# Retention and wave-MLP kernel: some transposes as four 64 by 64 tiles, and the order from the ninth unit on

## The chip, the cores and the metric

The kernel runs on one core of one Trainium2 chip. The metric is the device time of one execution in microseconds (us). The core has a matrix engine (PE, with PEld for its weight loads), three engines for elementwise work (DVE, ACT, POOL) and SP, which here only issues DMAs. ACT and POOL issue DMAs too.

## The reference, cut to what matters

Inputs are q, k and v (4 batches, 8 heads, 768 positions, 64 per head) and four weights. The first part is a linear recurrence per head, the second a token and channel mixer on the result.

```
gamma = 1.0 - 2.0 ** (-5.0 - arange(8));  scale = 1/8
for t in range(768):                                   # per batch and head
    state = gamma * state + outer(k[t], v[t])
    y[t] = scale * (q[t] @ state)
x = y, laid out as (4, 768, 512)
theta = x @ w_theta
zr, zi = x * cos(theta), x * sin(theta)
u = x + w_tok_r @ zr + w_tok_i @ zi                    # over the 768 positions
out = u + max(u @ w_ch, 0)
```

## The kernel before, in words

The recurrence is computed in blocks of 256 positions. A **unit** n is one block of 4 heads of one batch; there are 24, two (the halves of the heads) for each block, three blocks for each batch. Each pair of units yields two **tiles** C of 128 positions by 512 channels, 24 in all, and the second part works on these. Matrix work is in bf16 with f32 sums in PSUM.

The whole program is a list written out by hand, ORDER (L22 to L85): each token names a function and its arguments, and a loop at the end (L616) calls them one after the other. The last letter of a token, where there is one, names the engine (p POOL, v DVE, a ACT) or the DMA queue (s SP, a ACT). The instructions of one engine run in the order of the list; a layer below puts in the waits between engines, for data and for buffers that are used again.

For a unit: Lk, Lq, Lv load its k, q, v; ck, cq (or cqs) and cv cast and scale them into kqb and vb. Tk and Tq transpose k and q on PE, four 128 by 128 transposes each, into one PSUM tile kq_ps, and E copies that to kqT in SBUF. In some units one DMA transpose, Dk, issued by SP, takes the place of Tk, Tq and E. A computes the scores from kqT, m masks them on DVE. ST computes the new state terms, S0 and S1 (DVE or ACT) add them up, SB copies the state to a block-diagonal tile. I and Y add the parts of the output in PSUM (r_ps, tags R0 and R1), and XA or XB copies it to xT, transposed.

For a tile: Tx and Ex (or the DMA transpose Dx) turn xT back into x; Hh multiplies by w_theta; CN (ACT) takes cosine and sine, z multiplies. M.t.s adds one of six terms of the token mix of tile t, two matmuls with 512 columns; u adds x. Tu and Eu (or the DMA transpose Du) transpose u to uT; O multiplies by w_ch; f applies the maximum and the sum; SO stores. Tw and Ew transpose one tile of 128 rows of w_tok_r or w_tok_i, six transposes and a copy. The last tile and tile 20 are handled in halves (Mh, uh, Tuh, Euh, Oh, fh, Oa, fa).

A, ST and Y work on 64 by 64 pieces: 16 matmuls each, with 64 rows and 64 stationary columns, and a stream of 128 columns (A, Y) or 64 (ST). All other PE work uses the full 128 by 128 array.

PSUM buffers: tag tr (two) for kq_ps, x_ps, u_ps, w_ps and a few o_ps; tag acc (two) for th_ps, y_ps, o_ps; R0, R1 and at one each. In SBUF kqT has four buffers, kqb and vb five, xT, u and ot four, uT three.

Names and lines that matter below: L316 kq_ps transposes, L346 A, L373 ST, L423 Y, L411 I, L455 x_ps, L491 w_ps, L521 u_ps, L469 Hh, L509 M, L536 O, L137 and L139 copies on ACT and on the other engines, L157 loads, L332 Dk, L462 Dx, L531 Du, L547 SO.

Of the kernel before, what the change touches and what calls it, by code (L numbers as in the profile page):

```python
# [16 lines left out]
BF = mybir.dt.bfloat16  # L17
# [54 lines left out]
cv.21.v u.14 A.21 ST.21 CN.19.0 CN.19.1 S0.21.v M.15.3 M.15.5 S1.21 m.21 XA.20.1 Hh.18 CN.18.1
CN.18.0 Dx.18 Dk.22 ck.23.a M.15.4 M.15.2 SB.21.0.p M.15.1 M.15.0 SB.21.1.v Lv.23.s Du.12 Dx.19
XA.20.0 O.9 f.9 I.21 Y.21 A.22 ST.22 M.16.1 cqs.23.p u.15 m.22 S0.22.v z.18.p z.19.p M.16.5
SB.22.0.p M.16.4 O.12 M.16.0 SO.8.a M.16.2 M.16.3 SB.22.1.p XB.21.0.a XB.21.1.a SO.11.s Du.14
cv.23.p Dk.23 f.12 Du.13 Dx.20 Dx.21 Hh.21 u.16 I.22 A.23 Y.22 ST.23 CN.21.0 CN.21.1 Hh.20 CN.20.1
S0.23.v XA.22.1 XA.22.0 SB.23.0.a M.17.1 M.17.3 CN.20.0 M.17.0 SB.23.1.p I.23 M.17.2 m.23 Y.23 O.13
M.17.4 z.21.v M.17.5 Mh.0.1 Mh.0.3 XB.23.1.v f.13 Hh.23 u.17 XB.23.0.a SO.13.a CN.23.1 Du.16 Hh.22
z.20.v CN.22.1 Mh.0.2 M.19.3 Dx.23 CN.23.0 Dx.22 Mh.0.0 M.21.1 M.19.1 z.23.p CN.22.0 SO.6.a Du.17
M.18.1 O.16 M.21.2 M.19.2 M.19.0 M.18.3 f.16 SO.9.a M.18.5 z.22.p M.18.2 O.17 M.19.4 M.18.0 Mh.0.4  # L80
M.18.4 f.17 u.18 Du.15 SO.12.s O.15 M.19.5 f.15 u.19 SO.16.s M.22.2 M.22.1 O.14 Mh.0.5 uh.0 f.14
M.22.0 M.21.5 M.22.3 M.22.5 Du.19 M.21.4 SO.17.s M.22.4 Du.18 O.19 M.21.0 M.21.3 M.20.2 Mh.1.2
Mh.1.0 Mh.1.4 u.22 O.18 Mh.1.3 SO.15.a f.19 M.20.0 M.20.1 Tuh.0 u.21 Du.22 Du.21 f.18 M.20.3 Euh.0
M.20.4 Mh.1.1 M.20.5 u.20 O.22 Mh.1.5 uh.1 f.22 Tu.20 SO.14.a SO.19.s Eu.20.a O.21 SO.18.a Tuh.1
Euh.1 f.21 Oa.0 Oa.1 fa.0 fa.1 Oh.0 Oh.1 SO.21.a SO.22.s SO.20.s fh.0 SOh.0 fh.1 SOh.1 Z.31  # L85
# [14 lines left out]
def kernel(  # L100
# [228 lines left out]

    def Dk(n):  # L330
        kqT = work.tile([P, 2, 2, 2, P], BF, name="kqT", bufs=4)
        nc.sync.dma_start_transpose(  # L332
            out=kqT.rearrange("p w a j t -> p (w a j) t"),
            in_=st["kqb", n].rearrange("p w d -> p (w d)"))
        st["kqT", n] = kqT

    def A(n):
        kqT = st["kqT", n]
        at_ps = psum.tile([P, 2, 2, 2, P], FT, name="at_ps", tag="at", bufs=1)
        for j in range(2):  # L340
            for a in range(2):
                for c in range(2):
                    cols = slice(c * D, (c + 1) * D)
                    for g in range(2):
                        rows = slice(g * D, (g + 1) * D)
                        nc.tensor.matmul(at_ps[cols, g, j, a, :],  # L346
                                         kqT[rows, 0, a, j, cols],
                                         kqT[rows, 1, :, j, cols],
                                         start=(j == 0 and a == 0),
                                         stop=(j == 1 and a == 1), skip_group_check=True)  # L350
# [55 lines left out]
    def I(n):  # L406
        _, i, h = unit(n)
        r = R_of(n + 1)
        for c in range(0 if i else 1, 2):
            for j in range(2):  # L410
                nc.tensor.matmul(r[c][:, j * P:(j + 1) * P], sbd_of(n)[:, c, j, :],  # L411
                                 st["kqT", n][:, 1, :, j, c * D:(c + 1) * D],
# [47 lines left out]

# [186 lines left out]
```

## Time and profile before

| | us |
|---|---|
| median of 3 runs | 165.23 |
| lowest, highest | 165.05, 165.78 |
| span of the profiled execution | 163.6 |

The span runs from the first to the last instruction of one profiled execution; the time of the runs holds what lies around it as well. The profile page gives busy time by engine, the same in 40 slices of the span, DMA queues, and the groups of instructions by line, with the number of them, the time of all, the mean of one in ns, and the idle time of the engine ahead of them with what ended it. Matmuls are pipelined: the busy time of one (0.38 us for 512 columns) is longer than the distance to the next (0.22 us). Lines starting with L give the line of the kernel, then engine, operation and tiles as out<-in; SPq is SP's queue of DMA issues, where a row's length is the time of the issue.

### The profile page before, as it was taken

To read this page: it belongs to the slowest core of one execution; us is meant where nothing else is said; L and a number is where in the kernel's file an instruction comes from. 1 tells how busy PE (TensorE), PEld (TensorE's weight loads), DVE (VectorE), ACT (ScalarE), POOL (GpSimd) and SP (SyncE) were. 2 spreads that over 40 slices of the span, in tenths; PEclk is the share of its full clock that TensorE was granted. 3 is DMA by queue.
4 is the path that set the end of the run, shared out by engine and by line. 5 is a ranking of instruction groups with operands and counts; after the bars stand their busy time and mean duration, and the time that the engine had idled before them with its cause. 6 is when DMAs were issued, how large, how long until landed. Compare 5 with 4: busy or idle time off the path is not lost.

```text
span 163.6 us, 4928 instructions
## 1 busy us (share of the span) xinstructions
PE 155.2 (95%) x2034; PEld 87.2 (53%) x2034; DVE 114.0 (70%) x215; ACT 78.9 (48%) x140; POOL 74.3 (45%) x107
## 2 busy tenths in 40 slices
PE   5996889999999999999999999999999999999992
PEld 1453655656666655654554565554545554444561
DVE  3388687887994895984879894887867760345372
ACT  4976697974658255773343726732341616000020
POOL 7557389075034552730227599950469204600000
PEclk9999999999999999999999999999999999999999
DMA  3999999999999999999999999999897548515546
GB/s 115 297 290 255 268 283 236 275 220 286 220 162 232 223 291 139 338 203 270 324 263 198 134 268 221 242 193 298 125 245 136 103 92 227 160 64 128 129 164 224
DMA packets 69062, 34.93 MB, mean 214 GB/s; under 512 B 26416, under 2 KB 66096, under 8 KB 69040
## 3 DMA queue, kind: packets, MB, share of 16 engines
q1 hardware_dynamic: 56032, 23.73, 69.4%
q10 hardware_dynamic: 10320, 7.47, 17.7%
q0 software_dynamic: 2688, 3.41, 12.1%
q8 instruction: 16, 0.26, 0.7%
q14 instruction: 6, 0.05, 0.1%
HBM read 25.69 MB, written 6.29 MB: 196 GB/s over the span
## 4 chain that ended last, share of the span: by engine, by line
PE 76%; DMA 8%; ACT 5%; POOL 3%; issue 2%; SPq 2%; DVE 1%; POOLq 0%; ACTq 0%
PE y_ps L509 36%; PE o_ps L536 11%; PE th_ps L469 10%; DMA kqf<-in_k_dram 8%; PE r_ps L423 3%; ACT qx L233 3%; PE w_ps L491 3%; PE at_ps L346 3%; PE r_ps L411 2%; PE kq_ps L316 2%; SPq L157 2%; PE y_ps L561 2%; ACT cs L476 1%; PE x_ps L455 1%; PE r_ps L373 1%
## 5 line engine op out<-in xcount | busy, mean ns | idle before, releaser
L509 PE MATMUL y_ps<-z,wtr 128*128 128x512 bf16 x138 | 52.4, 380 | 0.0
L509 PE MATMUL y_ps<-z,wti 128*128 128x512 bf16 x138 | 52.3, 379 | 0.0
L483 POOL TENSOR_TENSOR z<-cs,x_sb 128x1024 bf16<-128x1024 bf16 x12 | 25.5, 2136 | 17.9 <-ACT cs L476 10.0
L355 DVE TENSOR_TENSOR at<-at_ps,mask 128x1024 bf16<-128x1024 f32 x24 | 29.2, 1216 | 0.2
L469 PE MATMUL th_ps<-wth,xT 128*128 128x512 bf16 x96 | 24.5, 379 | 0.5 <-ACT cs L476 0.4
L516 DVE TENSOR_TENSOR u<-y_ps,x_sb 128x512 bf16<-128x512 f32 x23 | 15.8, 688 | 12.7 <-PE y_ps L509 12.6
L542 DVE SCALAR_TENSOR_TENSOR ot<-o_ps,u 128x512 f32<-128x512 f32 x22 | 15.1, 688 | 12.5 <-PE o_ps L536 12.4
L308 POOL TENSOR_TENSOR vb<-vf,vsc 128x512 bf16<-128x512 f32 x15 | 15.6, 1041 | 17.3 <-DMA vf<-in_v_dram 16.9
L476 ACT ACTIVATE cs<-th_ps,zerob 128x512 bf16<-128x512 f32 x24 | 16.4, 685 | 13.3 <-PE th_ps L469 8.8
L536 PE MATMUL o_ps<-wch,uT 128*128 128x512 bf16 x88 | 22.6, 379 | 0.0
L476 ACT ACTIVATE cs<-th_ps,halfpi 128x512 bf16<-128x512 f32 x24 | 16.3, 686 | 11.5 <-issue 5.4
L509 PEld LDWEIGHTS <-wtr 128*128 128x128 bf16 x138 | 13.5, 98 | 12.7
L509 PEld LDWEIGHTS <-wti 128*128 128x128 bf16 x138 | 13.5, 98 | 12.0 <-issue 0.2
L139 POOL CAST sbd<-s 64x256 bf16<-64x256 f32 (+1 forms) x21 | 10.1, 481 | 20.8 <-DVE s L391 17.7
L137 ACT COPY kqT<-kq_ps 128x1024 bf16<-128x1024 bf16 x12 | 12.1, 1012 | 11.9 <-PE kq_ps L316 11.9
L469 PEld LDWEIGHTS <-xT 128*128 128x128 bf16 x96 | 8.8, 98 | 8.7 <-issue 0.5
L137 ACT CAST kqb<-kqf 128x512 bf16<-128x512 f32 x16 | 9.6, 620 | 6.9 <-DMA kqf<-in_k_dram 6.3
L536 PEld LDWEIGHTS <-uT 128*128 128x128 bf16 x88 | 8.1, 98 | 8.3
L278 PE MATMUL zz<-zero 128*128 128x512 bf16 x30 | 10.3, 476 | 1.9 <-DVE zero L192 1.9
L423 PE MATMUL r_ps<-at,vb 64*64 64x128 bf16 x384 | 9.9, 221 | 1.6 <-DVE at L355 1.6
L316 PE MATMUL kq_ps<-ident,kqb 128*128 128x128 bf16 x120 | 11.2, 220 | 0.3 <-POOL kqb L302 0.3
L139 POOL CAST kqb<-kqf 128x512 bf16<-128x512 f32 x12 | 7.2, 612 | 8.5 <-DMA kqf<-in_k_dram 8.4
(80 smaller groups left out, 208.7 us busy)
## 6 DMA issues: line engine op xcount, KB each, us to landing
vf<-in_v_dram SPq DMA_DIRECT2D x20, 256.0 KB, 5.9
kqf<-in_k_dram SPq DMA_DIRECT2D x19, 256.0 KB, 5.3
kqf<-in_q_dram SPq DMA_DIRECT2D x17, 256.0 KB, 5.8
out_dram<-ot ACTq DMA_DIRECT2D x12, 256.0 KB, 2.7
out_dram<-ot SPq DMA_DIRECT2D x11, 256.0 KB, 2.9
kqf<-in_q_dram ACTq DMA_DIRECT2D x7, 256.0 KB, 5.2
kqf<-in_k_dram ACTq DMA_DIRECT2D x5, 256.0 KB, 6.6
vf<-in_v_dram ACTq DMA_DIRECT2D x4, 256.0 KB, 5.8
```

The lines of the kernel that those rows point to most:

```text
L137: nc.scalar.copy(dst, src)
L139: engines[e].tensor_copy(dst, src)
L308: engines[e].tensor_mul(in_blocks(vb), by_token(raw["vf", n]), _bcast_last(K["vsc"][:, i, :, h * HU:(h + 1) * HU], D))
L355: nc.vector.tensor_mul(at.rearrange("p g j a t -> p (g j) (a t)"), st["at_ps", n].rearrange("p g j a t -> p (g j) (a t)"), _bcast_mid(K["m ...
L423: nc.tensor.matmul(st["R", n + 1][c][g * D:(g + 1) * D, j * P:(j + 1) * P], st["vb", n][rows, lo:lo + D], st["at", n][rows, g, j, a, :], s ...
L469: nc.tensor.matmul(th_ps, st["xT", C][:, j, :], K["wth"][:, j, :], start=(j == 0), stop=(j == 3))
L476: nc.scalar.activation(st["cs", C][:, w, :], st["th_ps", C], AF.Sin, bias=K["zerob" if w else "halfpi"], scale=1.0)
L483: engines[e].tensor_mul(st["z", b][:, c], st["cs", C], _bcast_mid(x_of(C), 2))
L509: nc.tensor.matmul(st["y", t], K["wT"][r][:, s0, t0 * P:(t0 + 1) * P], st["z", b][:, s0, r, :], start=(done == 0 and r == 0), stop=(done = ...
L516: nc.vector.tensor_add(st["u", t], st["y", t], st["x", b][:, t0, :])
L536: nc.tensor.matmul(o_ps, st["uT", t][:, j, :], K["wch"][:, j, :], start=(j == 0), stop=(j == nD - 1))
L542: nc.vector.scalar_tensor_tensor(st["ot", t], st["o", t], 0.0, st["u", t], ALU.max, ALU.add)
```

## The change

There are new functions that transpose in tiles of 64 by 64. tiles64 makes four transposes in place of one of 128 by 128; the two row halves go to two PSUM tiles (halves, both buffers of tag tr), and each half is copied out by itself. In kqT of such a unit the two halves of the positions lie in two separate parts, and kq_at picks the right view for A and I.

```
+    def tiles64(src, x0, x1, ps):
+        for x in range(x0, x1):
+            for c in range(2):
+                for r in range(2):
+                    rows = slice(r * D, (r + 1) * D)
+                    nc.tensor.transpose(ps[r][c * D:(c + 1) * D, x, :],
+                                        src[rows, x * P + c * D:x * P + (c + 1) * D],
+                                        K["ident"][rows, rows])
+
+    def halves(name, n):
+        return [psum.tile([P, n, D], BF, name=name, tag="tr", bufs=2) for _ in range(2)]
+
+    def kq6(n, w):
+        if ("kq6", n) not in st:
+            st["kq6", n] = halves("kq_ps", 8)
+        tiles64(st["kqb", n].rearrange("p w d -> p (w d)"), 4 * w, 4 * w + 4, st["kq6", n])
...
+    def E6(n, r, e):
+        if ("kqT", n) not in st:
+            st["kqT", n] = work.tile([P, 2, 2, 2, 2, D], BF, name="kqT", bufs=4)
+        copy(e, st["kqT", n][:, r].rearrange("p w a j t -> p (w a j) t"), st["kq6", n][r])
+
+    def kq_at(n, w, a, j, c):
+        if ("kq6", n) in st:
+            return st["kqT", n][:, c, w, a, j, :]
+        return st["kqT", n][:, w, a, j, c * D:(c + 1) * D]
...
-                                         kqT[rows, 0, a, j, cols],
-                                         kqT[rows, 1, :, j, cols],
+                                         kq_at(n, 0, a, j, c)[rows],
+                                         kq_at(n, 1, slice(0, 2), j, c)[rows],
...
-                                 st["kqT", n][:, 1, :, j, c * D:(c + 1) * D],
+                                 kq_at(n, 1, slice(0, 2), j, c),
...
+    def Tx6(C):
+        st["x6", C] = halves("x_ps", 4)
+        tiles64(st["xT", C].rearrange("p j t -> p (j t)"), 0, 4, st["x6", C])
+
+    def Ex6(C, r, e):
+        copy(e, x_of(C).rearrange("p (j e) -> p j e", j=4)[:, :, r * D:(r + 1) * D], st["x6", C][r])
...
```

Tk6 and Tq6 call kq6 for k and for q. Tw6 with Ew6 and Tu6 with Eu6 do the same for a weight tile and a u tile. They replace the old functions for the units 11, 14, 15 and 19, the tiles x 12 and 17, u 8 and 11, and the weight tile Tw.1.5.

The list ORDER is the same up to I.8 of the ninth unit (unit 8). From there on it has the same work, with the tokens above exchanged, in a new order; some copies, casts and products move to another engine. Here are the stretches of the new list that hold the new tokens (runs of tokens, shortened at both ends of a line).

```
+ ... Y.9 ST.10 Lk.14.s Lk.19.s f.2 A.10 Tw6.1.5 XB.9.0.a Lv.18.a cqs.12.p XB.9.1.a Ew6.1.5.1.a ...
+ ... Y.10 Eu.4.v Tk6.11 Lv.13.a Tq6.11 E6.11.0.v ST.11 E6.11.1.a S0.11.v Lv.12.s M.5.5 SO.1.a M.5.1 M.5.0 CN.9.1 Tu.3 A.11 ...
+ ... O.4 Tk6.14 Lq.15.s Tq6.14 Lq.16.s Y.11 ST.12 f.4 O.3 XA.11.0 SO.0.a E6.14.1.a Hh.10 E6.14.0.a ... A.12 ...
+ ... Tq6.15 Y.13 SO.2.s ST.14 Tk6.15 M.8.1 ... E6.15.1.v ... E6.15.0.v CN.13.1 Hh.12 Y.14 ST.15 Tx6.12 A.15 ...
+ ... Y.15 ST.16 cv.18.p Ex6.12.1.a Lv.23.s Ex6.12.0.a Tu6.8 XB.15.0.a A.16 f.6 u.10 Dk.17 z.13.p S0.16.v
+ M.11.2 SB.16.0.a SO.6.a XB.15.1.a m.16 Du.10 O.7 SB.16.1.p M.11.3 I.16 f.7 Y.16 ck.18.a Eu6.8.0.v ST.17
+ A.17 Hh.15 CN.15.0 Eu6.8.1.a z.12.p Tx.15 Lv.20.s M.11.0 XA.16.0 SO.7.s CN.15.1 S0.17.v M.11.5 SB.17.0.a
+ M.11.1 Dx.14 XA.16.1 SO.4.a M.11.4 m.17 Ex.15.v Hh.14 SB.17.1.p u.11 Dk.18 CN.14.0 I.17 Tu6.11 Y.17
+ CN.14.1 cq.20.p Eu6.11.0.v ST.18 O.10 S0.18.v XA.17.1 Hh.17 XA.17.0 Dx.16 S1.18 A.18 Eu6.11.1.v
+ SB.18.1.a SB.18.0.a Tq6.19 f.10 z.15.p Tk6.19 Lq.21.a CN.17.1 CN.17.0 E6.19.1.a O.8 I.18 Hh.16 m.18 f.8
+ O.11 SO.5.a z.14.p E6.19.0.v Lk.21.s CN.16.0 CN.16.1 cv.19.p ck.20.a Tx6.17 Y.18 A.19 f.11 ST.19 S0.19.a
+ Lk.22.s Ex6.17.1.a ck.21.a M.12.1 ck.22.a M.13.2 z.16.v M.13.3 S1.19 M.12.0 Lk.23.s SB.19.1.a cqs.21.v
+ XB.18.1.a M.12.3 M.12.2 Ex6.17.0.v XB.18.0.v z.17.v SB.19.0.p M.13.1 M.12.4 cv.20.v M.13.4 M.12.5 m.19
+ M.13.5 SO.10.s I.19 u.12 Y.19 ST.20 S0.20.v Dk.20 A.20 ...
```

The number of loads, stores and DMA transposes, and which units and tiles use a DMA transpose, are the same in both.

More of the change, by code (lines that the diff above doesn't have):

```diff
@@ new lines @@
+O.5 f.5 Tq6.15 Y.13 SO.2.s ST.14 Tk6.15 M.8.1 S0.14.v XA.13.1 M.8.4 cq.17.a u.8 ck.17.p Hh.13 S1.14
+M.10.0 SB.14.0.a cv.17.p M.10.2 E6.15.1.v SB.14.1.v XA.13.0 CN.13.0 ck.19.p M.10.5 cqs.18.v Lv.21.s
+cv.15.p I.14 E6.15.0.v CN.13.1 Hh.12 Y.14 ST.15 Tx6.12 A.15 CN.12.0 CN.12.1 cv.16.v cq.19.v S0.15.v
+Dk.16 SB.15.0.p Dx.13 M.10.3 XB.14.0.a S1.15 M.10.1 Lv.19.a O.6 M.10.4 XB.14.1.a m.15 SB.15.1.p I.15
+Y.15 ST.16 cv.18.p Ex6.12.1.a Lv.23.s Ex6.12.0.a Tu6.8 XB.15.0.a A.16 f.6 u.10 Dk.17 z.13.p S0.16.v
@@ L86 @@
+M.21.0 Du.22 O.19 SO.17.s M.21.5 Mh.1.4 M.20.2 O.18 f.19 M.20.1 M.20.0 Mh.1.1 Mh.1.3 SO.14.a u.21 Tuh.0
+M.20.5 f.18 M.20.4 SO.19.s M.20.3 O.22 u.20 Du.21 f.22 Mh.1.2 Tu.20 Mh.1.0 uh.1 Euh.0 O.21 Eu.20.a Tuh.1
+SO.18.a Oa.0 Oa.1 f.21 fa.0 Euh.1 fa.1 Oh.0 Oh.1 SO.21.a SO.22.s SO.20.s fh.0 SOh.0 fh.1 SOh.1 Z.31
 """.split()
@@ L492, in Tw, with Tw6, Ew6 @@
         st["w_ps", r, t0] = w_ps
+    def Tw6(r, t0):
+        g = sum(t0 >= hi for _, hi in groups)
+        st["w6", r, t0] = halves("w_ps", nT)
+        tiles64(K["row"][r][g][:, t0 - groups[g][0]], 0, nT, st["w6", r, t0])
+    def Ew6(r, t0, x, e):
+        copy(e, K["wT"][r][:, :, t0 * P + x * D:t0 * P + (x + 1) * D], st["w6", r, t0][x])
     def Ew(r, t0, e):
@@ L527, in Eu, with Tu6, Eu6 @@
         copy(e, st["uT", t], st["u_ps", t])
+    def Tu6(t):
+        st["u6", t] = halves("u_ps", nD)
+        tiles64(st["u", t], 0, nD, st["u6", t])
+    def Eu6(t, r, e):
+        if ("uT", t) not in st:
+            st["uT", t] = work.tile([P, nD, P], BF, name="uT", bufs=3)
+        copy(e, st["uT", t][:, :, r * D:(r + 1) * D], st["u6", t][r])
     def Du(t):
```

111 lines of the change are left out of this document (48 added, 63 removed).

## The prediction

> **What bounds the kernel now.** I read the page first: the span, the busy shares and the row of PE in 40 slices.
>
> ```profile
> span 163.6 us, 4928 instructions
> ...
> PE 155.2 (95%) x2034; PEld 87.2 (53%) x2034; DVE 114.0 (70%) x215; ACT 78.9 (48%) x140; POOL 74.3 (45%) x107
> ...
> PE   5996889999999999999999999999999999999992
> ```
>
> PE is full from the seventh slice on, and no other engine comes near it over the span. A full digit could still hide a few per cent, and matmuls overlap, so the second view is the busy time by stretch, from 48 us (where the two orders part) to 158 us (the last four groups). Its columns are the stretch, its length, the busy time of PE, PEld, DVE, ACT and POOL with their instructions, the granted clock and the DMA load.
>
> ```profile
> 64.00:80.00 16.00, 15.91 (x203) 8.80 (x201) 12.46 (x22) 9.45 (x17) 5.05 (x5) 1.00 1.11 271
> ...
> sum 110.00, PE 109.86 PEld 59.60 DVE 74.57 ACT 43.83 POOL 47.66; mean PE 15.69 PEld 8.51 DVE 10.65 ACT 6.26 POOL 6.81
> ```
>
> In these 110 us PE lacks 0.14 us, at full clock (1.00 in the quoted stretch). DVE is busy 68% of it, ACT 40%, POOL 43%. So the time after 48 us is the sum of what PE is given, and the change is worth what it takes from that sum, less any wait that the new order brings. PE starts each matmul when the one before has streamed, so the price of a group is the distance from its start to the next group's start, not its busy time. The third view is PE's timeline, read that way (first column start, second length; a group of one M token is two matmuls).
>
> ```profile
> 38.26 0.61 PE L316 MATMUL kq_ps<-ident,kqb 128*128 128x128 bf16 x8
> 38.70 0.38 PE L509 MATMUL y_ps<-z,wtr 128*128 128x512 bf16 x1
> ...
> 39.77 0.42 PE L423 MATMUL r_ps<-at,vb 64*64 64x128 bf16 x16
> 40.02 0.29 PE L373 MATMUL r_ps<-vb,kqb 64*64 64x64 bf16 x16
> 40.14 0.40 PE L346 MATMUL at_ps<-kqT 64*64 64x128 bf16 x16
> 40.47 0.39 PE L509 MATMUL y_ps<-z,wtr 128*128 128x512 bf16 x1
> ```
>
> ```profile
> 64.11 0.38 PE L509 MATMUL y_ps<-z,wtr 128*128 128x512 bf16 x1
> 64.33 0.38 PE L509 MATMUL y_ps<-z,wti 128*128 128x512 bf16 x1
> 64.64 0.42 PE L346 MATMUL at_ps<-kqT 64*64 64x128 bf16 x16
> 64.88 0.39 PE L423 MATMUL r_ps<-at,vb 64*64 64x128 bf16 x16
> ...
> 66.57 0.39 PE L316 MATMUL kq_ps<-ident,kqb 128*128 128x128 bf16 x4
> 66.80 1.03 PE L536 MATMUL o_ps<-wch,uT 128*128 128x512 bf16 x4
> 67.66 0.39 PE L411 MATMUL r_ps<-kqT,sbd 128*128 128x128 bf16 x4
> ```
>
> Full transposes: eight in 0.44 us (38.26 to 38.70), 0.055 each. Groups of 64-row work: Y (L423) 0.25, ST (L373) 0.12, A (L346) 0.24 where other 64-row work follows (64.64 to 64.88). One large matmul 0.22 (64.11 to 64.33), four 0.86 (66.80 to 67.66), an M token 0.43, I (four of L411) as four transposes, 0.22. A change of tiling costs: from M into A 0.31 in place of 0.22 (64.33 to 64.64), so 0.09 in; A with M behind it 0.33 (40.14 to 40.47) in place of 0.24, so 0.09 to 0.10 out. Once in and out is 0.19 to 0.2 us.
>
> **The change: PE.** Removed are 8 transposes for each of units 11, 14, 15 and 19 (32), 4 for each of two x and two u tiles (16), 6 for the weight tile: 54 at 0.055 is 2.97 us. Each becomes four of 64 by 64: 216 transposes. The trace has no such transpose. The nearest row is ST: 64 rows, a 64 by 64 stationary tile, 64 moving columns, the same loop over two row halves and two column halves with two PSUM tiles as targets, 16 in 0.12, or 0.0075 each. From above the row of Y bounds it (the same tiles with twice the moving columns, 16 in 0.25). I take ST, since all three sizes agree: 216 x 0.0075 = 1.62 us; the upper end is 3.4 us. I see no reason for less than ST, whose 64 columns must stream too.
>
> Where they stand decides what else they cost. I counted in both orders the runs of 64-row work that lie between other PE work: 33 before and 36 after, from 48 us on 17 and 20. Every group of new transposes shares a run with other 64-row work (Y.10, Tk6.11, Tq6.11, ST.11 is one). The three more come from A.11, A.12 and A.18: each shared the run of a Y and an ST, and now stands in one of its own, A.18 with Tq6.19 and Tk6.19 behind it. Three runs at 0.2 are 0.6 us. PE sum: -2.97 + 1.62 + 0.6 = **-0.75 us**.
>
> The Trainium skill (TensorEngine Tiling (Array Packing), Key Properties) says that changing the tiling mode drains TensorE; this trace puts a price of 0.2 us on a round trip, and it is this rule that takes back nearly half of the gain. The same page (Instruction Overhead) gives each matmul some 60 cycles of overhead and advises against tiling a dimension that is already small; the ST row speaks against that, for 16 of them in 0.12 us leave 7.5 ns for each. What it would do here is the third rival below.
>
> **The copies.** A unit's E was one ACT copy of 1024 columns; it becomes two of 512, on ACT or DVE. The other tiles go the same way.
>
> ```profile
> L137 ACT COPY kqT<-kq_ps 128x1024 bf16<-128x1024 bf16 x12 | 12.1, 1012 | 11.9 <-PE kq_ps L316 11.9
> L137 ACT COPY uT<-u_ps 128x512 bf16<-128x512 bf16 x4 | 2.3, 586 | 3.8 <-PE u_ps L521 3.7
> L139 DVE COPY uT<-u_ps 128x512 bf16<-128x512 bf16 x3 | 1.2, 417 | 0.0
> L139 DVE COPY s<-r_ps 128x128 f32<-128x128 f32 x5 | 1.4, 287 | 1.7 <-PE r_ps L373 1.7
> ```
>
> Four E of 1.01 on ACT (4.05 us) become four halves on ACT (2.34) and four on DVE (1.67). For a DVE copy of 256 columns the bounds are 0.29 (s) and 0.42 (uT). All moves of work between DVE, ACT and POOL together change none of the three by more than some tenths of a us, on engines that are idle a third of the time or more. I cost them at nothing, and PE's other work is the cover: between Tq6.11 and A.11 lie ST.11, three M and Tu.3, 0.12 + 1.29 + 0.22 = 1.6 us, for two copies side by side of 0.59 and 0.42. Without that cover A.11 would wait 0.6 us.
>
> The halves also take both PSUM buffers of tag tr, so the next transpose waits for two copies. The thinnest cover is at Tu6.11: till Tq6.19 PE does Y.17, ST.18, O.10, Hh.17 and A.18 (0.25 + 0.12 + 0.86 + 0.86 + 0.24, with two changes 2.6 us), while DVE does Eu6.11.0, S0.18, two XA, S1.18 and Eu6.11.1, about 0.29 + 0.29 + 0.42 + 0.42 + 0.29 + 0.29 = 2.0 us (S0 and S1 as the row of s, XA as a 512-column copy). It holds by 0.6 us, less the latencies between engines.
>
> **The queues.** The number of DMAs is the same and their order is not. Two places count. The first is Dk.18, the DMA transpose that A.18 needs.
>
> ```profile
> 91.85 1.56 SPq L332 DMA_TRANSPOSE kqT<-kqb  x1
> 93.47 1.25 SPq L157 DMA_DIRECT2D kqf<-in_k_dram  x2
> 94.83 1.27 SPq L531 DMA_TRANSPOSE uT<-u  x1
> 96.20 1.21 SPq L462 DMA_TRANSPOSE x_sb<-xT  x1
> 97.46 0.57 SPq L157 DMA_DIRECT2D vf<-in_v_dram  x1
> ```
>
> ```profile
> L332 SPq DMA_TRANSPOSE kqT<-kqb x9: 1237/1961/2992, 60.1 to 123.2; - x9
> ...
> DMA to landing us min/median/max: 4.1/4.6/6.4
> ```
>
> ```profile
> L355 DVE TENSOR_TENSOR at<-at_ps,mask 128x1024 bf16<-128x1024 f32 x24 | 29.2, 1216 | 0.2
> L542 DVE SCALAR_TENSOR_TENSOR ot<-o_ps,u 128x512 f32<-128x512 f32 x22 | 15.1, 688 | 12.5 <-PE o_ps L536 12.4
> ```
>
> Before, Dk.18 (91.85) was issued ahead of Du.10 and Dx.14 and had landed long before A.18. In the new order it stands behind Du.10, Lv.20, SO.7 and Dx.14, and SO.7 waits for f.7, which waits for O.7. Counted from the end of O.7: f.7 behind the rest of m.16 (1.22 us, begun before O.7 ends; I put the rest at 0.4), f.7 0.69, SO.7 0.57 (as a load), Dx.14 1.21: Dk.18 is issued at 2.9 us and lands 4.1, 4.6 or 6.4 later, at 7.0, 7.5 or 9.3. PE's work from O.7 to A.18 is five M (2.15), I.16, I.17 and Tx.15 (0.66), Hh.15, Hh.14, O.10 and Hh.17 (3.44), the run Y.16 ST.17 A.17 (0.8) and the run Tu6.11 Y.17 ST.18 (0.7): 7.75 us. At the median the transpose is in time by 0.2, at the slowest it is 1.6 late. I take the median, so nothing.
>
> The second is Lk.21, Lk.22 and Lk.23, which now stand behind Dx.16, and Dx.16 waits for XA.17.0. Behind the casts ck.21 and ck.22 ACT has SB.19.1 and XB.18.1, and I.19 waits for both.
>
> ```profile
> kqf<-in_k_dram SPq DMA_DIRECT2D x19, 256.0 KB, 5.3
> ...
> L137 ACT CAST kqb<-kqf 128x512 bf16<-128x512 f32 x16 | 9.6, 620 | 6.9 <-DMA kqf<-in_k_dram 6.3
> ```
>
> From the end of Y.17: S0.18 and two XA 1.1, Dx.16 1.2, Lk.21 and Lk.22 issued at 2.3 and 2.9, landed at 7.6 and 8.2, casts to 8.8, the two small ACT copies (under the 0.59 of 512 columns; I take 0.4 each) to 9.6. PE till I.19 has O.10, Hh.17, O.8, Hh.16, O.11 (4.3), eleven M (4.7), half an I (0.1), and the rest of one run and two others (0.2 + 0.7 + 0.9): 10.9. In time by 1.3; a load 1.3 slower than the median would be felt.
>
> **The sum.** The span of the profiled execution was 163.6 us; the median of the runs, 165.23, is 1.6 us above it, which I take as fixed. Start and tail keep their instructions (up to I.8, and the last four groups of PE work). Span 163.6 - 0.75 = 162.8, time **164.5 us**, 0.45% less. The 0.14 us that PE lacked may go or double, so this case alone reaches from 164.3 to 164.9.
>
> **Rivals.**
> - *More gain: the gaps close too.* 165.23 - 0.75 - 0.14 = 164.3, and a cheaper round trip (0.17 in place of 0.2) takes another 0.1: 164.2. For it: engine loads are unchanged, and half copies free the tiles earlier. Against: the gaps are small already.
> - *The DMA transposes come late.* Dk.18 lands after A.18's turn, PE stands, and everything behind moves by as much. It costs from a landing of 4.8 us on; at 6.4 us 1.6, and Dk.20 behind the three loads and SO.10 has the same cause. Net -0.75 + 1.6 = 166.1, with half as much again at Dk.20 166.9. For it: kqT transposes took longer than the median while the DMA engines were full. Against: ahead of Dk.18 fewer loads are in flight in the new order.
> - *The small transposes do not overlap.* If one alone takes half of a full one (64 columns for 128), 0.028, then 216 take 6.0, and the sum is -2.97 + 6.0 + 0.6 = +3.6: 168.9. With the row of Y it is -2.97 + 3.4 + 0.6 = +1.0: 166.3. For it: no run shows a transpose in tiles. Against: ST overlaps and has the same shape. The overhead of 60 cycles for each matmul (the Trainium skill, TensorEngine Tiling (Array Packing), Instruction Overhead) would bring about this case if it were paid one after the other.
> - *The gain doesn't arrive:* small waits spread over the new order give back 0.5 to 1.2 us: 165.0 to 165.7. With PE this full, any wait that isn't hidden shows.
>
> **Chances.** About half a per cent, 0.83 us, is what can be told from no change: below 164.40 is faster, above 166.06 slower. Forecast as summed, 0.3; more gain 0.3; gain given back in small waits 0.17; late DMA transposes 0.16; no overlap 0.07. The first case lies on both sides of 164.40 (a quarter of it faster), and of the late ones a fifth stay under 166.06. So faster 0.3 + 0.08 = 0.38, slower 0.13 + 0.07 = 0.20, the rest, 0.42, no change. The range leaves out the top of the last two rivals and a tenth at the lower end: 164.0 to 166.3.
>
> **What would show it.** A group of 16 small transposes with 0.12 us to the next start says that the term is right, 0.25 or more that it isn't. PE busy in the stretches of 16 us should stay 16.0. The waits of PE for kqT by a DMA transpose, at A.18 or A.20, would be the late transposes, and a wait of a transpose for a copy (tag tr) the doubled halves. It is wrong if PE idles more than 0.8 us from 48 us on, or if the 64-row runs cost more than 0.2 us each.

## The result, and the profile after

The changed kernel takes 168.09 us (median; 167.06 to 168.88), the kernel before 165.47 on the same chip: ratio 1.0166, 95% interval 1.0132 to 1.0199. It is slower, and 168.09 lies outside the predicted range of 164.0 to 166.3. (Ratios leave disturbed executions out, so some differ a little from the quotient of two medians.)

The page of after: the span, PE's busy time and PE in 40 slices.

```profile
span 166.4 us, 5231 instructions
...
PE 152.6 (92%) x2168; PEld 85.7 (51%) x2196; DVE 114.7 (69%) x216; ACT 78.4 (47%) x149; POOL 73.7 (44%) x106
...
PE   5996889999999999989799999699999999999992
```

The profiled execution took 168.07, so here too some 1.7 us lie around the span, which is 2.8 us longer than before's. PE was full in before; now three slices fall to 8, 7 and 6. The stretches of after say the same in us (columns as in the prediction; the last row is the sum from 48 to 158 us):

```profile
64.00:80.00 16.00, 15.26 (x202) 7.92 (x202) 11.80 (x21) 6.90 (x14) 5.58 (x6) 1.00 1.24 252
80.00:96.00 16.00, 14.44 (x289) 7.85 (x285) 11.15 (x22) 6.45 (x17) 9.10 (x13) 1.00 1.20 249
96.00:112.00 16.00, 14.11 (x267) 7.89 (x270) 11.53 (x26) 9.77 (x21) 9.07 (x8) 1.00 1.11 219
...
sum 110.00, PE 105.01 PEld 56.49 DVE 73.67 ACT 42.72 POOL 45.07; mean PE 15.00 PEld 8.07 DVE 10.52 ACT 6.10 POOL 6.44
```

PE lacks 4.99 us of 110 where it lacked 0.14, at the same clock of 1.00, and DVE, ACT and POOL are no busier than before. So it isn't work that was added; PE waits, and far more than the 0.8 us that the prediction named as a sign of being wrong. The waits of PE in after from 48 us on (us in total, times, longest):

```profile
PE at_ps L376 <- DMA kqT<-kqb: 1.6, 1, 1.6
PE y_ps L554 <- issue: 1.1, 7, 0.2
PE r_ps L403 <- POOL vb L306: 1.0, 1, 1.0
PE th_ps L506 <- DVE ot L596: 0.5, 1, 0.5
```

Three are single waits. The row of "issue" is none: its 0.16 us each stand ahead of groups whose first matmul has no record, so 1.1 of the 4.99 us are no wait. PE's timeline of after around the three, and around O.7:

```profile
70.73 0.42 PE L376 MATMUL at_ps<-kqT 64*64 64x128 bf16 x16
71.69 1.02 PE L506 MATMUL th_ps<-wth,xT 128*128 128x512 bf16 x4 [0.53 <-DVE ot L596]
...
79.68 0.42 PE L453 MATMUL r_ps<-at,vb 64*64 64x128 bf16 x16
81.13 0.32 PE L403 MATMUL r_ps<-vb,kqb 64*64 64x64 bf16 x16 [1.03 <-POOL vb L306]
...
95.40 1.03 PE L590 MATMUL o_ps<-wch,uT 128*128 128x512 bf16 x4
...
103.29 1.03 PE L506 MATMUL th_ps<-wth,xT 128*128 128x512 bf16 x4
105.89 0.42 PE L376 MATMUL at_ps<-kqT 64*64 64x128 bf16 x16 [1.57 <-DMA kqT<-kqb]
106.14 0.42 PE L333 MATMUL kq_ps<-ident,kqb 64*64 64x64 bf16 x32
106.49 1.04 PE L590 MATMUL o_ps<-wch,uT 128*128 128x512 bf16 x3
```

From start to next start, against the prices of before: A.12 to Hh.11 0.96 for 0.33, so 0.63 lost; Y.12 to ST.13 1.45 for 0.25, 1.20 lost; Hh.17 to A.18 2.60 for 0.86 + 0.09, 1.65 lost. Together 3.48; less the 0.75 that PE's sum was to shrink by it is 2.73 of the 2.8 us. What stands behind each:

*Hh.11.* It waits for a PSUM buffer that f.3 (DVE) reads, and f.3 waits for an ot buffer that a store holds. The queue rows of after, the store SO.1 on ACT and its landing, and f.3 on DVE:

```profile
62.58 0.36 ACTq L601 DMA_DIRECT2D out_dram<-ot  x1
```

```profile
DMA to landing us min/median/max: 8.3/8.3/8.3
```

```profile
70.94 0.69 DVE L596 SCALAR_TENSOR_TENSOR ot<-o_ps,u 128x512 f32<-128x512 f32 x1 [1.61 <-DMA out_dram<-ot]
```

The other stores that after issues from 63 to 112 us landed in 3.1 to 6.8 us; this one took 8.3, and f.3 started as it landed, 62.58 + 8.3 = 70.9.

*ST.13.* It needs vb of unit 13 from cv.13, which POOL runs third behind ck.15 and cv.14. POOL's rows of after:

```profile
78.34 0.73 POOL L137 CAST kqb<-kqf 128x512 bf16<-128x512 f32 x1 [7.77 <-PE y_ps L554]
79.04 2.04 POOL L306 TENSOR_TENSOR vb<-vf,vsc 128x512 bf16<-128x512 f32 x2
```

POOL stands 7.77 us at ck.15. The view names PE, but no PE work feeds a cast; what ck.15 needs is the load Lk.15, which SP issued at 72.23 and which took 6.0 us: 78.2. The two vb behind it end at 81.08, and ST.13 starts at 81.13. Before issued Lk.15 near 54 us already, and its cast stood on DVE; the new order has moved the load by some 18 us and put its cast ahead of cv.13.

*A.18.* SP's rows of after: SO.7, Dx.14 and then Dk.18.

```profile
97.18 0.45 SPq L601 DMA_DIRECT2D out_dram<-ot  x1
97.72 1.25 SPq L499 DMA_TRANSPOSE x_sb<-xT  x1
99.08 2.95 SPq L363 DMA_TRANSPOSE kqT<-kqb  x1
```

Dk.18 is issued at 99.08 (91.85 in before) and A.18 can start at 105.89, 6.8 us later. Its own landing has no record, so A.18's start stands for it. The DMA transposes to kqT whose landing is on record, from issue to landing (before 4.1/4.6/6.4):

```profile
DMA to landing us min/median/max: 3.2/5.3/8.8
```

All three waits are DMAs that land late. The small transposes are as cheap as forecast: 32 of them in 0.25 us (PE's timeline of after, Tk6.11 and Tq6.11).

```profile
62.00 0.42 PE L333 MATMUL kq_ps<-ident,kqb 64*64 64x64 bf16 x32
62.25 0.31 PE L403 MATMUL r_ps<-vb,kqb 64*64 64x64 bf16 x16
```

### The profile page after: what moved, and what is told of

Its sections match the earlier page's. It is cut to its first block, busy times and chain, and to the rows that moved or that the text cites. A ratio compares the mean times of both kernels' runs of the same rounds, so it can differ in the third digit from the quotient of the medians.

```text
span 166.4 us, 5231 instructions
## 1 busy us (share of the span) xinstructions
PE 152.6 (92%) x2168; PEld 85.7 (51%) x2196; DVE 114.7 (69%) x216; ACT 78.4 (47%) x149; POOL 73.7 (44%) x106
## 4 chain that ended last, share of the span: by engine, by line
PE 74%; DMA 12%; DVE 5%; POOL 3%; issue 2%; ACT 1%; DVEq 0%; POOLq 0%; ACTq 0%
PE y_ps L554 32%; PE o_ps L590 10%; PE th_ps L506 10%; DMA out_dram<-ot 5%; PE r_ps L453 4%; DMA kqT<-kqb 4%; PE at_ps L376 4%; DMA kqf<-in_q_dram 3%; PE kq_ps L314 3%; PE r_ps L441 2%; PE w_ps L528 2%; DVE at L385 2%; PE r_ps L403 2%; PE y_ps L615 2%; POOL vb L306 1%
## 5 line engine op out<-in xcount | busy, mean ns | idle before, releaser
L554 PE MATMUL y_ps<-z,wti 128*128 128x512 bf16 x132 | 50.0, 379 | 1.5 <-issue 1.4
L554 PE MATMUL y_ps<-z,wtr 128*128 128x512 bf16 x128 | 48.6, 379 | 0.2
L520 POOL TENSOR_TENSOR z<-cs,x_sb 128x1024 bf16<-128x1024 bf16 x11 | 23.5, 2136 | 16.2 <-ACT cs L513 9.0
L306 POOL TENSOR_TENSOR vb<-vf,vsc 128x512 bf16<-128x512 f32 x17 | 19.2, 1130 | 13.5 <-DMA vf<-in_v_dram 11.0
L135 ACT CAST sbd<-s 64x256 bf16<-64x256 f32 (+1 forms) x27 | 9.9, 368 | 13.6 <-DVE s L421 11.9
L137 POOL CAST kqb<-kqf 128x512 bf16<-128x512 f32 x16 | 9.7, 619 | 13.3 <-PE y_ps L554 7.8
L137 POOL CAST sbd<-s 64x256 bf16<-64x256 f32 (+1 forms) x15 | 5.5, 364 | 22.5 <-DVE s L421 18.6
L135 ACT COPY kqT<-kq_ps 128x1024 bf16<-128x1024 bf16 (+1 forms) x11 | 9.3, 858 | 8.8 <-PE kq_ps L314 6.7
L520 DVE TENSOR_TENSOR z<-cs,x_sb 128x1024 bf16<-128x1024 bf16 x13 | 9.8, 757 | 3.9 <-ACT cs L513 2.1
L376 PE MATMUL at_ps<-kqT 64*64 64x128 bf16 x384 | 9.8, 219 | 2.0 <-DMA kqT<-kqb 1.6
```

What stands on the lines that cost most here:

```text
L135: nc.scalar.copy(dst, src)
L137: engines[e].tensor_copy(dst, src)
L306: engines[e].tensor_mul(in_blocks(vb), by_token(raw["vf", n]), _bcast_last(K["vsc"][:, i, :, h * HU:(h + 1) * HU], D))
L376: nc.tensor.matmul(at_ps[cols, g, j, a, :], kq_at(n, 0, a, j, c)[rows], kq_at(n, 1, slice(0, 2), j, c)[rows], start=(j == 0 and a == 0), s ...
L520: engines[e].tensor_mul(st["z", b][:, c], st["cs", C], _bcast_mid(x_of(C), 2))
L554: nc.tensor.matmul(st["y", t], K["wT"][r][:, s0, t0 * P:(t0 + 1) * P], st["z", b][:, s0, r, :], start=(done == 0 and r == 0), stop=(done = ...
```

## The experiments

Each run was compared with before on the same chip; rows can come from different chips, where before's median was 165.37 to 165.56. Starting kernel, median and ratio to before:

| run | from | median us | ratio to before, 95% |
|---|---|---|---|
| e1_dk18 | after | 167.09 | 1.0114, 1.0077 to 1.0152 |
| e2_cv13 | after | 168.43 | 1.0189, 1.0151 to 1.0226 |
| e3_ot5 | after | 168.75 | 1.0192, 1.0158 to 1.0227 |
| e4_all | after | 168.29 | 1.0157, 1.0118 to 1.0195 |
| e5_loads | after | 170.64 | 1.0294, 1.0256 to 1.0332 |
| e6_loads_dk | after | 172.20 | 1.0380, 1.0337 to 1.0423 |
| e7_before_early | before | 167.25 | 1.0098, 1.0062 to 1.0134 |
| e8_before_tiles | before | 167.64 | 1.0131, 1.0111 to 1.0152 |
| e9_before_tiles2 | before | 165.69 | 1.0016, 0.9996 to 1.0036 |
| e10_lv22 | after | 166.96 | 1.0051, 1.0021 to 1.0080 |
| e11_before_dk18 | before | 170.70 | 1.0328, 1.0282 to 1.0373 |
| e12_dx13 | before | 165.97 | 1.0028, 1.0016 to 1.0040 |

### One wait removed at a time (e1, e2, e3)

e1 issues Dk.18 ahead of Lv.20:

```
- ... Tx.15 Lv.20.s M.11.0 ... SB.17.1.p u.11 Dk.18 CN.14.0 ...
+ ... Tx.15 Dk.18 Lv.20.s M.11.0 ... SB.17.1.p u.11 CN.14.0 ...
```

> One token moved in the changed kernel: Dk.18 stands ahead of Lv.20, SO.7 and Dx.14 on SP's queue in place of behind them. Theory (late DMAs): in the changed kernel PE stood 1.65 us at A.18 until Dk.18 landed at 104.94 us; issued some 2.8 us earlier (96.3 in place of 99.08) it lands in time, and the time falls by 1.3 to 1.65 us to about 166.5. Rival (the small transposes or their copies are what costs): the wait at A.18 goes and the time stays within 0.4 us of 168.1. Rival (the DMA engines are simply full, waits only move): A.18 starts earlier and another wait of 1 us or more appears behind it, time 167.5 or more.

It took 1.0 us off the median of after (168.09 to 167.09), less than the theory's 1.3 to 1.65, and the two spreads overlap (167.06 to 168.88 and 166.62 to 168.82). PE's waits from 48 us on in e1:

```profile
PE r_ps L404 <- POOL vb L307: 1.0, 1, 1.0
PE th_ps L507 <- DVE ot L597: 0.5, 1, 0.5
```

The wait of A.18 is gone, the other two stand as they were. Dk.18 is now issued at 97.22 and lands 4.4 us later. (The landing at 104.94 that the expectation gives for after is that of a store, SO.4, issued on ACT at 99.05.) So the place of Dk.18 on SP costs about 1 us of the 2.6.

e2 puts cv.13 ahead of ck.15 on POOL:

```
- ... Eu.5.v ck.15.p M.7.2 ... Lq.19.a cv.13.p Lv.15.s ...
+ ... Eu.5.v cv.13.p ck.15.p M.7.2 ... Lq.19.a Lv.15.s ...
```

> One token moved in the changed kernel: cv.13 on POOL stands ahead of ck.15 and cv.14 in place of behind them. Theory: ck.15 blocks POOL until Lk.15 lands (78.3 us), and ST.13 waits 1.2 us for cv.13 behind it; with cv.13 first that wait goes, and the time falls by 0.8 to 1.2 us to about 167. Rival (copies or tiles cost): unchanged within 0.4 us. Rival (waits only move): PE waits as much at a later place, A.18 above all, 167.7 or more.

e3 gives ot a fifth buffer (`bufs=4` to `bufs=5` at both places).

> The changed kernel with five buffers for ot in place of four, nothing else. Theory: f.3 waited 1.6 us for the store SO.1 to give its buffer back, and Hh.11 stood 0.45 us behind it; with a fifth buffer f.3 starts on time and the time falls by 0.3 to 0.5 us to about 167.7. Rival: f.3 was late for its own data or its place in DVE's order; then nothing changes.

Neither gained. The long idle times of PE in e2, in its timeline from 48 us on, are these two:

```profile
50.95 0.33 PE L404 MATMUL r_ps<-vb,kqb 64*64 64x64 bf16 x16 [1.96 <-POOL vb L307]
100.92 0.42 PE L377 MATMUL at_ps<-kqT 64*64 64x128 bf16 x16 [1.58 <-DMA kqT<-kqb]
```

ST.13 no longer waits, but A.17 does (1.58), for Dk.17. The wait at 50.95 (ST.9) is in no other trace; this execution took 170.12 where the median is 168.43. Behind that wait the clock was lower too, 0.50 from 52 to 54 us. The same view of e3:

```profile
77.87 0.38 PE L554 MATMUL y_ps<-z,wtr 128*128 128x512 bf16 x1 [1.49 <-DVE z L520]
98.95 0.42 PE L376 MATMUL at_ps<-kqT 64*64 64x128 bf16 x16 [0.71 <-DMA kqT<-kqb]
```

Hh.11's wait is gone, and 1.49 us at an M (z.11, late because Dx.11 is) and 0.71 at A.17 have come. PE arrives earlier at the next transfer that is late.

### The three together (e4), and the loads put back (e5, e6, e10)

e4 is e1, e2 and e3 in one.

> The three edits together (Dk.18 early, cv.13 early, five buffers for ot). Theory: all three waits go, 1.65 + 1.2 + 0.45 = 3.3 us, and what is left is PE's sum, 0.7 us under the kernel before: 164.6 to 165.2. Rival (copies or tiles cost): 167.5 or more. Rival (waits only move, the DMA engines are full): 166 to 167.5, with PE waiting at other DMAs.

PE's long idle times in e4:

```profile
77.44 0.38 PE L555 MATMUL y_ps<-z,wtr 128*128 128x512 bf16 x1 [1.48 <-DVE z L521]
98.53 0.42 PE L377 MATMUL at_ps<-kqT 64*64 64x128 bf16 x16 [0.99 <-DMA kqT<-kqb]
```

The three waits have gone and two of the same kind have taken their place: Dx.11 took 7.3 us to land and Dk.17 6.7. The median, 168.29, is that of after: the theory of three separate mishaps (164.6 to 165.2) fell, and the rival of moving waits had its sign but expected 166 to 167.5. What is left to vary is when the transfers are put into the queues. The new order issues Lv.22, Lk.19 and Lv.18 between 49 and 57 us, far ahead of their use; in before they come after 82 us. e5 moves the three later, and e6 also moves Dk.18 (as e1) and Dk.17 earlier:

```
- ... Lv.11.s Lv.22.s CN.7.1 ... Lk.14.s Lk.19.s f.2 ... XB.9.0.a Lv.18.a cqs.12.p ...
+ ... Lv.11.s CN.7.1 ... Lk.14.s f.2 ... XB.9.0.a cqs.12.p ...
+ ... Du.6 Lk.19.s Lq.19.a Lv.18.a cv.13.p ... S0.19.a Lv.22.s Lk.22.s ...
```

> The changed kernel with three loads moved back: Lv.22 to just ahead of Lk.22, Lk.19 behind Du.6, Lv.18 behind Lq.19. The new order issues 15 DMAs from 48 to 60 us where the old one issues 10, and from 60 to 72 us its DMAs take 7.3 us (median) to land in place of 5.8. Theory (loads fetched too early delay what is due): SO.1, Lk.15 and Dx.11 land 1 to 2 us earlier, the waits at Hh.11 (0.6) and ST.13 (1.2) shrink or go, A.18 keeps its wait; time down by 1 to 1.8 us, 166.4 to 167.1. Rival (each wait is a matter of its own place in a queue): the waits at Hh.11, ST.13, A.18 stay, time within 0.4 us of 168.1. Rival (the small transposes or their copies): the same, unchanged.

> The loads moved back as before this, and Dk.18 ahead of Lv.20, SO.7 and Dx.14, Dk.17 right behind Dk.16. Theory: no wait of PE above 0.3 us is left, and the time is PE's sum, 164.6 to 165.3, under the kernel before (165.4). Rival (waits only move, since the DMA engines are full whatever the order): 166 to 167.5, with PE waiting for other DMAs. Rival (the tiles cost): 167 or more without visible waits.

Both are slower than after. e5 freed the stretch up to 82 us as expected (none of the three waits is left), and jammed the next one. PE's two longest idle times in e5, and POOL's row ahead of the last:

```profile
95.07 0.42 PE L377 MATMUL at_ps<-kqT 64*64 64x128 bf16 x16 [0.87 <-DMA kqT<-kqb]
99.55 0.40 PE L442 MATMUL r_ps<-kqT,sbd 128*128 128x128 bf16 x4 [2.23 <-POOL sbd L138]
```

```profile
96.92 2.12 POOL L521 TENSOR_TENSOR z<-cs,x_sb 128x1024 bf16<-128x1024 bf16 x1 [3.82 <-DMA x_sb<-xT]
```

Dk.16, whose issue held SP for 4.7 us, landed after 9.1, and behind it in the queue Dx.13 came late for POOL, and through POOL for PE. In e6 Dk.17 stood ahead of Dx.13 as well, and the same wait grew to 2.88. Not all of the loss is waiting: behind the 2.23 us of e5 the clock was 0.50 from 101 to 103 us.

e10 keeps e1's and e2's edits and of the loads moves Lv.22 alone:

```
- ... Lv.11.s Lv.22.s CN.7.1 ...
+ ... Lv.11.s CN.7.1 ... S0.19.a Lv.22.s Lk.22.s ...
```

> After, with Dk.18 ahead of Lv.20 on SP, cv.13 ahead of ck.15 on GpSimd, and of the early loads Lv.22 alone moved back to ahead of Lk.22; Lk.19 and Lv.18 stay early. Theory (the load issued early into the stretch from 52 to 62 us is what makes the later ones late, and one load less there is felt): the wait of Hh.11 (0.6) goes or halves, none takes the place of ST.13's, A.17 waits 0.3 to 1; 165.8 to 166.6. Rival (waits only move, as when the three edits stood together): 167.5 to 168.5 with a wait of over 1 us on an x or k transpose at another place.

166.96, the lowest median in the new order by little (e1 has 167.09 on another chip), a little above the range that was expected; its runs reach from 164.93 to 168.61, and the profiled one took 167.65. Its long idle times:

```profile
81.26 0.42 PE L377 MATMUL at_ps<-kqT 64*64 64x128 bf16 x16 [0.97 <-DMA kqT<-kqb]
98.15 0.42 PE L377 MATMUL at_ps<-kqT 64*64 64x128 bf16 x16 [0.59 <-DMA kqT<-kqb]
```

The two are again DMA transposes. Hh.11 waits only 0.2, but not because its store came sooner: SO.1 took 8.1 us to land, f.3 waited 1.56 for it, and Hh.11 started at 71.67 (71.69 in after); PE came there later, since A.12 ahead of it waited 0.26. So this trace doesn't show that one early load less is felt where the theory put it, and what the lower median comes from is open, as is where the other two loads should stand.

### The queue edits done to before (e7, e11)

If the queues are the cause, before must get slower from them without a single tile. e7 moves only the three loads early in before's order; e11 moves only Dk.18 behind SO.7:

```
e7   - ... Lv.18.a M.8.5 ...  Lk.19.s Lk.20.s ...  Tx.15 Lv.22.s SO.7.s ...
     + ... M.3.2 Lv.22.s Dx.7 ...  Lk.14.s Lk.19.s Y.9 ...  Lv.11.s Lv.18.a XB.9.1.a ...
e11  - ... M.10.2 Dk.18 O.6 ...  Lv.22.s SO.7.s M.11.0 ...
     + ... M.10.2 O.6 ...  Lv.22.s SO.7.s Dk.18 M.11.0 ...
```

> The kernel before, with the same three loads (Lv.22, Lk.19, Lv.18) moved to where the new order has them; no tiles, nothing else. Theory (early loads): DMAs issued from 55 to 75 us land later by 1 us or more, and PE waits somewhere for 0.3 to 1.5 us; time 165.7 to 167. Rival: the old order has enough slack everywhere, time within 0.3 us of 165.4.

> Before, with one DMA transpose moved: Dk.18 to behind SO.7 on SP, where it stands in after; no tiles, no other move. Theory (a Dk.18 issued behind Dx.14 and SO.7 lands too late for A.18): issue at 98 to 99.5, landing at 103 to 105, TensorE waits 1.5 to 2.5 before A.18; 166.8 to 167.6, ratio 1.008 to 1.013. Rival (in before's traffic it lands in some 3 us and the median was right to use): landing before 102, wait under 0.5; 165.2 to 165.8.

e7's 167.25 lies a little above the expected 165.7 to 167. PE's one long idle time in e7 from 48 us on, and what POOL waited for ahead of it:

```profile
67.53 0.32 PE L371 MATMUL r_ps<-vb,kqb 64*64 64x64 bf16 x16 [1.45 <-POOL vb L306]
```

```profile
66.43 1.04 POOL L306 TENSOR_TENSOR vb<-vf,vsc 128x512 bf16<-128x512 f32 x1 [5.47 <-DMA vf<-in_v_dram]
```

Three loads brought forward push back the load that is needed next, and PE pays 1.45 us at ST.11. (This span is 2.3 us longer than before's; 0.8 of that was lost at the start, ahead of the first moved load.) And PE's longest wait in e11, with the two rows at its end:

```profile
PE at_ps L344 <- DMA kqT<-kqb: 6.1, 1, 6.1
```

```profile
106.79 0.64 PE L344 MATMUL at_ps<-kqT 64*64 64x128 bf16 x16 [6.13 <-DMA kqT<-kqb]
107.22 0.64 PE L421 MATMUL r_ps<-at,vb 64*64 64x128 bf16 x16
```

Dk.18 was issued at 99.84 and landed 6.9 us later, at the moment when A.18 starts (106.79). The median of e11 is 5.3 us above before, about three times what was expected: the direction held, the size didn't. A landing at 103 to 105 was expected and it came at 106.7; before's A.18 comes at 100.40, and each us of lateness behind that counts whole, so that already the expected landing meant 2.6 to 4.6 and not 1.5 to 2.5. A second loss was in no sum: behind the wait the clock is 0.50 from 106 to 110 us, and A takes 0.43 us to the next start where it took 0.24. The profiled execution took 172.97, 2.3 above the median, so its 6.1 isn't the median's wait; but all six executions of e11 have a mean clock of 0.98 or 0.99.

This second loss shows only behind long waits: in the traces of e2, e5 and e11, whose longest waits are 1.96, 2.23 and 6.13 us, the clock falls to 0.50; in after it stays at 1.00, with no wait above 1.57. What decides isn't shown: the profiled execution of e6 kept 1.00 behind its 2.88, while its other five have a mean of 0.98 to 0.99.

### The tiles without the queue edits (e8, e9, e12)

e8 takes before's order and makes two u tiles and one weight tile in 64 by 64 pieces, with the copies where they stood:

```
- ... ST.9 Tw.0.3 ... A.17 Tu.8 Hh.15 ... ck.21.p Eu.8.a ... u.11 Tu.11 A.18 ... SB.18.1.p Eu.11.v ...
+ ... ST.9 Tw6.0.3 ... A.17 Tu6.8 Hh.15 ... ck.21.p Eu6.8.0.a Eu6.8.1.a ... u.11 Tu6.11 A.18 ... Eu6.11.0.v Eu6.11.1.v ...
```

> The order of the kernel before with three groups as 64 by 64 tiles, those that stand next to 64-row work there: Tu.8, Tu.11 and Tw.0.3, copies in halves on the engine of the old copy. No other token moves. Theory (a small transpose costs what ST does, 0.125 per 16, and adds no change of tiling): PE's sum falls by 0.1 + 0.1 + 0.15 = 0.35 us; time 165.0 to 165.2. Rival (tiles cost more than they save): 165.4 or more, and a group of 16 with more than 0.2 us to the next start.

PE's timeline in e8 at Tu6.8 and at the transpose that comes next in tag tr:

```profile
96.25 0.29 PE L334 MATMUL u_ps<-ident,u 64*64 64x64 bf16 x16
96.48 1.04 PE L507 MATMUL th_ps<-wth,xT 128*128 128x512 bf16 x4
...
99.19 0.38 PE L486 MATMUL x_ps<-ident,xT 128*128 128x128 bf16 x4 [1.24 <-ACT uT L136]
```

16 small transposes and the change back take 0.23, as summed; but the halves hold both tr buffers till the two copies at Eu6.8, and Tx.15 waits 1.24 us for them. Tq.19 behind Tu6.11 waits in the same way for its copies, 0.39 (at 105.00). So e8 is 2.2 us above before, where the theory had 0.2 to 0.4 less and the rival a dearer transpose. That cost is real where copies stand late. The changed kernel places them early, and has no such wait.

e9 has tiles in five places of before's order (weight tile 0.3, x tiles 8 and 12, k and q of unit 14, u tile 8; with k and q apart they are the six runs of the expectation), each copy early enough. Two of the five, shortened:

```
- ... ST.11 CN.9.1 ... Dk.12 Tx.8 Tq.14 O.4 ... I.11 Tk.14 Ex.8.v A.12 Y.11 ST.12 f.4 ...
+ ... ST.11 Tx6.8 CN.9.1 ... Dk.12 O.4 ... I.11 Ex6.8.0.v Ex6.8.1.v A.12 Y.11 ST.12 Tk6.14 Tq6.14 f.4 ...
```

> The order of before with six runs of tiles beside the rows of 64 that stand there: weight tile 0.3 in front of ST.9's shared order, x of unit 8 behind ST.11, k and q of unit 14 behind ST.12, x of unit 12 behind ST.15, u of unit 8 behind A.17; every copy out of a pair of tr buffers stands where the next two transposes have them in time. No load and no DMA transpose is moved. Gain of TensorE by the rows: 0.10 to 0.19 a run, 0.64 in all. Theory (the tiles pay as summed where they touch neither the queues nor the tr buffers): 164.6 to 165.0, ratio 0.995 to 0.998, no wait of TensorE over 0.5 after 50 us. Rival (a pair of halves holds both tr buffers and so costs more than it saves wherever it is put): 166 to 168, with waits on uT, xT or kqT copies in the rows. Rival (the queues are so tight that any shift of 0.1 us moves a wait): one wait on a transposed tile of 0.5 to 1.5 at a place without tiles, 165.5 to 166.5.

165.69, no difference that can be measured, and none of the 0.64 gained. Part of it goes at A.12 (PE's timeline of e9, then DVE's; this execution took 166.32, 0.6 above the median):

```profile
67.23 0.61 PE L442 MATMUL r_ps<-kqT,sbd 128*128 128x128 bf16 x4
67.88 0.42 PE L377 MATMUL at_ps<-kqT 64*64 64x128 bf16 x16
```

```profile
66.61 1.22 DVE L386 TENSOR_TENSOR at<-at_ps,mask 128x1024 bf16<-128x1024 f32 x1
```

Four matmuls of I and the change of tiling are worth 0.22 + 0.09; here it is 0.65 to the next start, and A.12 begins 0.05 us after DVE has emptied the scores of the unit ahead (66.61 + 1.22 = 67.83). PE came 0.3 us early and stood. More goes at a DMA transpose: Dx.13 landed 5.8 us after its issue at 91.30, POOL's z.13 came late, and I.18 waited 0.8.

```profile
PE r_ps L442 <- POOL sbd L138: 0.8, 1, 0.8
```

e12 is e9 with Dx.13 ahead of Du.7 on SP, the last attempt at a kernel that beats before.

> The six runs of tiles in the order of before (as in the run e9_before_tiles2), with one more edit: on SP the DMA transpose of x of unit 13 (Dx.13) stands ahead of that of u of unit 7 (Du.7). In e9_before_tiles2 Dx.13 landed at 97.05 us against 94.90 in before, and GpSimd and VectorE waited 0.9 us each for it, which TensorE paid with 0.76 before I.18. Theory (that wait is the one thing that eats the tiles' gain): Dx.13 lands by 95.5, both waits go, 164.7 to 165.2, ratio 0.994 to 0.999 to before. Rival (the transposes on SP are so tight that the wait moves to Du.7 or Dk.18): a wait of 0.4 to 1.5 before O.7 or A.18; 165.4 to 166.5.

That wait fell to 0.2 and the profiled span from 164.6 to 164.0 us, but the median is 165.97, slower than before by 0.3%, and not the 164.7 to 165.2 of the theory; the rival had the time (165.4 to 166.5), but its wait at O.7 or A.18 isn't in the trace. A.12 stands in this trace as in e9 (0.65 to the next start), and the small transposes of the weight tile wait 0.23 for a copy; the two are 0.57 of the 0.64. No kernel that was tried beats before.

## Why the prediction was wrong

The step that failed is the term of the waits for DMAs, which the sum put at nothing: it was 3.48 us, at three places, of which the prediction had weighed one and dropped it. PE's own sum, the other half, came out.

*PE's sum: right.* Small transposes were priced at 0.12 for 16 and took 0.125 (32 in 0.25). A round trip through the tiling was priced at 0.2; A.18's own run shows an exit of 0.10 (32 transposes, 106.14 to 106.49, 0.35 less 0.25). With the waits taken off, the span shrank by 3.48 - 2.8 = 0.7 us, where -0.75 stood (that is the subtraction above once more; the proof is the rows). The third rival (no overlap) is refuted, and with it the reading of the Trainium skill (TensorEngine Tiling (Array Packing), Instruction Overhead) by which each small matmul pays its overhead alone: 7.8 ns each is what the rows show.

*The copies: right for this order.* No wait for a copy out of tr appears in after. e8 shows that the cover which the prediction named is needed: without it, 1.24 and 0.39 us.

*Dk.18: the term that was mis-sized.* "I take the median, so nothing." The issue was worked out well: 2.9 us after the end of O.7; it was 99.08 - (95.40 + 0.86) = 2.8. PE's work up to A.18 was put at 7.75 and was 103.29 + 0.95 - 96.26 = 8.0. The landing was put at 4.6 and was 6.8, beyond even the slowest (6.4) of the trace of before. The term was to be 1.6 late at worst and was 1.65; in e1, with Dk.18 early, the wait is gone and the median 1.0 lower. The rival of the late DMA transposes had the mechanism and the price, at a chance of 0.16. The median was also taken over the wrong stretch: it holds transposes issued after 105 us, which landed in 4.1 to 4.4. The three that before issues from 83 to 92 us, Dk.18 among them, took:

```profile
DMA to landing us min/median/max: 4.7/5.5/6.4
```

With 5.5 the prediction's own sum has A.18 waiting 2.9 + 5.5 - 7.75 = 0.65 us.

*"Two places count": wrong.* Two more were missed, a store that holds ot (0.63) and a load at the head of POOL's line (1.20). They aren't late by their own place alone, though Lk.15 is issued 18 us later than in before. e7 shows that the three early loads by themselves cost 1.8 us of the median in before's order, and I had not costed moved loads at all unless a reader stood right behind them. What a load brought forward pushes back was not in the sum.

*"Ahead of Dk.18 fewer loads are in flight": not so.* When Dk.18 was issued, one load, two stores and one transpose were on record as still to land in after, the last at 105.0 us; in before one load, one store and one transpose, the last at 95.8. The DMA load in the stretches from 64 to 112 us is over 1.1 in both kernels (1.24, 1.20, 1.11 in after; 1.11, 1.17, 1.27 in before); with queues this full, a landing time taken from one order isn't one of another order.

*"The gain doesn't arrive" and e4:* with PE and the DMA engines both full, a wait removed showed up again one transfer further on (e2, e3, e4, e6), and PE's own saving went the same way in e9. The time to land goes with the stretch: in after the transposes to kqT issued from 61 to 92 us took 5.4 to 8.8, those after 110 us (the DMA load is 0.84 and less from 112 us on) 3.2 to 5.2. Which of the transfers ahead of one counts wasn't separated; nor was an order found in which the three loads do no harm. The new order also moves casts and copies between engines, and no run moves those alone.

## What to carry to other kernels

A full engine doesn't mean that its work alone sets the time: ask what comes next behind it, and if DMA queues are as full, cost each moved transfer at the slowest landing of the stretch where it will stand, not at the median of the trace, and each load brought forward at what it pushes back. Try an edit of the arithmetic in the old order first (e9), and the order edit on the old arithmetic (e7, e11): that parts the two in two runs. Removing a wait is worth its length only if nothing else lands in the time after it.

## What was not expected of the hardware

A DMA transpose can hold its queue far longer than the 1.2 us that its issue takes at best: 4.7 us for Dk.16 in e5, and 2.95 for Dk.18 in after, so that all DMAs behind it on SP shift too. Loads do it too: 2.43 us for Lv.22 in e11. And the store of one 128 by 512 tile, 2.3 us (SP) or 2.5 (ACT) to land at the median of after, took 8.3 when issued among loads at 62.58 us. Behind a long wait of PE the granted clock can fall to half: 0.50 in e2, e5 and e11, as told above.
